# A two-layer attention stack on one NeuronCore: another table for the order, engines and buffers of the same operations

## The chip, the cores and the metric

The kernel runs on one core of a Trainium2 chip. A core has engines with instruction streams of their own: PE (TensorE, matrix products), ACT (ScalarE), DVE (VectorE), POOL (GpSimd) and SP (SyncE, which here only issues transfers). They meet at semaphores. The metric is the device time of one execution in microseconds. The kernel before took 455.38 us in the median of three runs (454.83 to 461.96).

## The reference

One sequence of 2048 rows of 512 elements in bf16 goes through four blocks A, B, A, B, each behind a layer norm and added to its input. Both have 32 heads of 16 columns.

```python
# A: attention in 4 segments of 512 rows, with a memory M, z carried from segment to segment
logits = einsum('bhqd,bhkd->bhqk', qs, ks) * scale + mask     # causal inside the segment
p = softmax(logits); a_dot = einsum('bhqk,bhkd->bhqd', p, vs)
num = einsum('bhld,bhde->bhle', phi(qs), M)                    # phi(t) = t+1 if t>0 else exp(t)
den = einsum('bhld,bhd->bhl', phi(qs), z)[..., None] + 1e-06
o = g * num / den + (1.0 - g) * a_dot                          # g = sigmoid(beta), per head
M = M + einsum('bhld,bhle->bhde', phi(ks), vs); z = z + sum_l phi(ks)
# B: linear attention over all 2048 rows
phi_q = concat(softmax(q @ w_phi), softmax(-q @ w_phi)); phi_k likewise
kv = einsum('bhsf,bhsd->bhfd', phi_k, v); z = sum_s phi_k
o = einsum('bhqf,bhfd->bhqd', phi_q, kv) / (einsum('bhqf,bhf->bhq', phi_q, z) + 1e-06)
# after either: x = x + o @ wo
```

## The kernel before

The program is written as a graph of 2904 operations. `Graph.op` records for each the engines that may run it, what it reads and writes, and the tiles it opens; nothing is sent to an engine then. Helpers do the recording, so most instructions of the profile carry a helper's line:

- `mm` (L326) records a group of matrix products: scores S and Sd (pK, pQ), probabilities times values PV (pW, and p or pP), the normaliser Zq (Rz) and numerator N (Rkv) of block B's queries.
- `pair` (L341) records a projection in two operations, one for each half of the contraction; between them PE may run other products. The second half carries a wait on the first (`hard=o1`).
- `act` (L351) is an ACT function, nearly always an exponential out of PSUM. `evac` copies PSUM to SBUF on ACT (L359) or on DVE (L360): this is the main choice of engine that the table has. `kmask` (L686 DVE, L688 ACT) and the memsets at the start (POOL or DVE) have such a choice too.
- `tr` (L364) is a transposing transfer on SP; `tpe` (L380) a transposition by PE with an evacuation. `dma` (L368) writes the value rows to DRAM (v_rows) and brings them back spread over partitions (pW). `load` (L462) brings the inputs and weights in, WB_o, the last layer's output weight, in eight pieces.
- L795 adds a segment's memory (Macc), L961 is a residual sum, L1015 and L1012 sum the keys' weights, L929 is block B's transposition with its sum (otp), whose evacuation is called ote; otr is the transposition of an output, xnT that of a normed input (xnTe its evacuation), Km the key mask, Kev and Vev the evacuations of keys and values, BVe that of block B's values, BK, BV, BQ and Wo the projections.

Work is tiled in 128 rows by up to 1024 columns. PSUM is four tiles of 128 x 1024 f32 (D0 to D3); nearly every product goes through one of them, so a product can start only when the reader of that tile's last use is done. A of a segment, B's keys of the segment, then B's queries of all segments together with the next layer's first projections follow each other, and the table interleaves them.

`Graph.place` decodes the table: a global order of the operations, an engine for each, and a buffer for each tile. A tile that takes over a buffer must wait for the last users of the one before it (`t.base`). `Graph.emit` then cuts the global order into five streams, one for each engine, and gives each operation the waits that the orders so far don't already cover:

```python
order = [self.ops[i] for i in np.frombuffer(raw, "<u2", n)]
slots = dict(zip(tiles, raw[3 * n:]))
    o.seq, o.eng = k, ENGS[raw[2 * n + o.id]]
...
cand = [d for d in deps if (d is o.hard or not (d.kind == "c" and d.eng == "pe" and e == "pe")) and not covers(kn, d)]
```

Every engine, SP's transfers included, goes through its stream in order: an instruction that waits holds all that stand behind it.

Of the kernel before, what the change touches and what calls it, by code (L numbers as in the profile page):

```python
# [16 lines left out]
D = 512  # L17
H = 32
# [42 lines left out]
class Tile:  # L61
# [17 lines left out]
    @property  # L79
    def t(self):  # L80
        return self.pool.tensors[self.slot]
# [1125 lines left out]
c-q~01C%YvvUWtIvs$OSk8RtwZQHhO+qP}nwr$&fRlCpJnYnk?y!+O_-oMs;xqDYuRz^lfeDOu>tkrRVL1IV_0QI0g5Hx^>&<LVIV`u_Rp&2xXWDp(VLOiGjnV~wAhxkweBxHk<Py<Rq  # L1207
R%ih&p%o~o3AvyGRD^<12y#MeXal987PN&jPzl;W3@8f;pfD7H_Rs-pLs38|1~H*Bl!M~X5n@3d=mec1AtZwAkOQhfUFZ!dAr)BY0=Xdxe1{+K6RN^%2!uD_Krr-yx6l_1e1z067}CHX
0PG3_;3**Xhj-8qy1@__3Q6G^aOe&LAvfm1_wWfm!xtC@d9erdgo%(3d%-l!iNhcl22lp^1H$z%12@2Q3`c`dz)YMA&*23O#t9GvmOemn%m}&IJa`GOU?Y^kuP_|Oz$WO2{V|wAXex|`
qF4+^!Z%m~4n=}3Fb#&_e8|E!!*&<}L(z}6LP?wsJ760`qX9SvRzWHBCx**lCuD)yFbQYEK->iyRs+XbFc||eEzE!^7=%k9I*o<Xum;NGR1|1&5|qUPxEzXLK`e|FFdXK`wJ;3JVLm8>  # L1210
XQ4E%gF?6hD&k5Qj`MH?#-K_V4#vTJ91j675+}oc9EDThFzkl|cmy1bKnLI;B*f7eKt~}MBhnr?2{CCe&cWTV4`*Q_j75>i4`<^7*b9j<KkS1EI0iGpSk$O+F)YO;I2RjW6I_gouo^bR
g_sVSVpLd()$u$mz{6-TB}OKRXJ8fXqKP;T7r}Tez?R{1Jc3nlH>JWxSQ%?z3P_Dru`$NRwOA9Qz(qJf>o5vkfJ+buS5bXT$7*41tcwew9yZ5=6c^LOYKo76R0mt&IoOOXu^G0)E!Y}Q
;wjvSo6sMUV0es&$MFQV!M1n^{4oTh(sc->qZoh@@CNLm^SA@EvIH0rFW@oUircXr?xo|f4WnZkTtk=P3be<A7!5-)Hm#-b)B$(nYCMN~Fa{ojLwFX~;Ck$cJ@5>6!VTD(R$wGNjXg0L
uArTmo@HQdXcxxBmb8*mP-pCd4e26Y!pIm4yJCGxj@>XNMa5Rsi1twpN<}HK0bRzV7>D*#FYJwduqL&o+EkZnQ9FuDQLqjbWc6qX#iQJ;J6?q=cnvyJV!A;$X(@G~tGJ0aQv$k%*YPek
rzX^xhEgXQM$M=%wx=6-6K`P%+<|-8fjUwP8crjqDRrf5^cd4(H@c74X(Yv`6EKRN-~-HxPcb9Dz=!w@vtcGIK$-C+X2;&thk8;kDoCeb5GAB#G=Y{=dc2K~Fas8%@$?+W&^Q`MqbVJB
r~cHJ22ej*M`I}om7pWEo`%q1I!YVp4i=`8l!x7djg*Z|q)C*Wm7-&GoDNYA)`Jey7D`H~X&X(Zt@Ie4KoR<ciRc}D#*8d4drx0*I~8Kz@fGI4T=W+2P(GHM^3V@FOH=48zM<E+gU--h
+DRv<Fnde)=p@~z+famEp=30bp3!M4%F@s&x=P>h9G$02G>x9qbh=Ep=n%`qa<bc$kKW@0I?O&%F?vK<@Dlq>KauDuy}`@uF{Put^om~72TV^#*hf6d($YivK}G2+eW3jGg)&eFmYIE|
($tY9r@`zA{iGpmAmfyuU1NjT3lcPsGSWM|&fM}vFX;xGPYdWKW7L&(W8dfkNy-b~Nzp~hN(WeR%0$4BX<A6xs4O#dkPT%g*f3U(on&RHCmYE|u@P(r^<v#wZ$@l58^g-89;_l8&B{|5
%1*b~ZN}IDR)J2jiqwboW96tX%L6&75@n%dtUo)=j<cCGi)Pb4wx1PaIcO}q!ZK5FHjZ6ol6PWfSP7>1ImX#Nc8AR&!S1tCtTL5klD%R6>>+!=?y^Pnmd$04*hMyvy<&4IfZc>D^q9S7
# [80 lines left out]
```

## Time and profile before

| | before |
|---|---|
| runs, us | 454.83, 455.38, 461.96 |
| median, us | 455.38 |
| profiled execution: its span, us | 454.8 |
| instructions | 26184, of them 12085 products and 12085 weight loads on PE |
| busy: PE, ACT, DVE, POOL | 427.2, 420.9, 403.1, 58.4 us |

The span is that of the profiled execution, which has no time of its own beside it; it lies 0.6 us under the median. Times inside it count from its start. Busy times of one engine are the sum of its instructions, overlaps of pipelined products counted once. In rows of instructions, out<-in are tile names with the buffer's number left out; "[0.73 <-PE D L326]" says that the engine had been idle 0.73 us and what ended that: here a product of line 326 into a PSUM tile. "issue" stands where the profile shows nothing that was waited for. In rows of groups, the numbers behind the count are the busy time in us, the mean of one in ns, and the idle time just before them.

### The profile page before, as it was taken

To read this page: it belongs to the slowest core of one execution; us is meant where nothing else is said; L and a number is where in the kernel's file an instruction comes from. 1 tells how busy PE (TensorE), PEld (TensorE's weight loads), DVE (VectorE), ACT (ScalarE), POOL (GpSimd) and SP (SyncE) were. 2 spreads that over 40 slices of the span, in tenths; PEclk is the share of its full clock that TensorE was granted. 3 is DMA by queue.
4 is the path that set the end of the run, shared out by engine and by line. 5 is a ranking of instruction groups with operands and counts; after the bars stand their busy time and mean duration, and the time that the engine had idled before them with its cause. 6 is when DMAs were issued, how large, how long until landed. Compare 5 with 4: busy or idle time off the path is not lost.

```text
span 454.8 us, 26184 instructions
## 1 busy us (share of the span) xinstructions
PE 427.2 (94%) x12085; PEld 289.5 (64%) x12085; DVE 403.1 (89%) x766; ACT 420.9 (93%) x584; POOL 58.4 (13%) x146
## 2 busy tenths in 40 slices
PE   8999999999999989989999998999999988999787
PEld 4756667767766666655556666677677666765444
DVE  7999999998798978869999997999898896788897
ACT  5999999999999997899999999999899999699992
POOL 3411014010101101100330112020020020110000
PEclk9999999999999999999999999999999999999999
DMA  8976655564247212101255668436232414300355
GB/s 251 217 165 100 99 93 109 107 87 80 45 76 111 38 40 50 13 3 27 62 111 86 85 97 103 71 87 81 57 50 49 109 19 63 46 17 4 49 91 180
DMA packets 105167, 36.71 MB, mean 81 GB/s; under 512 B 91730, under 2 KB 105058, under 8 KB 105058
## 3 DMA queue, kind: packets, MB, share of 16 engines
q1 hardware_dynamic: 104226, 34.50, 42.9%
q8 instruction: 95, 1.56, 1.4%
q10 hardware_dynamic: 800, 0.52, 0.4%
q14 instruction: 14, 0.11, 0.1%
q0 software_dynamic: 32, 0.02, 0.0%
HBM read 10.76 MB, written 6.55 MB: 38 GB/s over the span
## 4 chain that ended last, share of the span: by engine, by line
PE 61%; ACT 20%; DVE 12%; issue 3%; DMA 3%; POOL 1%; DVEq 0%
PE D L341 38%; PE D L326 22%; ACT p L351 11%; ACT pP L351 7%; DVE X L961 2%; DVE pQ L686 1%; DVE p L1117 1%; DVE stats L599 1%; DMA pX<-p 1%; DMA p<-p 1%; ACT pS L351 1%; DVE p L620 1%; DMA X<-in_A_x_dram 1%; DVE pK L360 1%; DVE p L906 1%
## 5 line engine op out<-in xcount | busy, mean ns | idle before, releaser
L351 ACT ACTIVATE p<-D 128x1024 bf16<-128x1024 f32 (+1 forms) x256 | 225.6, 934 | 10.8 <-PE D L341 4.9
L351 ACT ACTIVATE pP<-D 128x640 bf16<-128x640 f32 (+2 forms) x192 | 149.5, 828 | 7.2 <-PE D L326 5.9
L326 PE MATMUL D<-pK,pQ 64*128 64x128 bf16 (+6 forms) x1792 | 112.0, 227 | 4.2 <-ACT p L351 1.0
L326 PEld LDWEIGHTS D<-pK,pQ 64*128 64x128 bf16 x1792 | 67.0, 93 | 40.2 <-ACT pP L351 8.5
L326 PE MATMUL D<-pW,pP 64*128 64x50 bf16 (+1 forms) x3072 | 84.0, 181 | 3.4 <-issue 2.7
L326 PEld LDWEIGHTS D<-pW,pP 64*128 64x128 bf16 x3072 | 68.6, 93 | 9.2 <-issue 3.8
L607 POOL TENSOR_SCALAR rstd<-mv 128x1 f32<-128x1 f32 x60 | 17.0, 288 | 340.8 <-DVE mv L600 340.4
L326 PE MATMUL D<-pW,p 64*128 64x50 bf16 (+1 forms) x2048 | 50.4, 181 | 0.4 <-DVE pQ L686 0.2
L326 PEld LDWEIGHTS D<-pW,p 64*128 64x128 bf16 x2048 | 44.3, 93 | 3.9 <-issue 1.1
L599 DVE BATCH_NORM_STATS2 stats<-X 128x6 f32<-128x512 bf16 x63 | 42.3, 679 | 1.9 <-DMA X<-in_A_x_dram 1.6
L961 DVE TENSOR_TENSOR X<-X,D 128x1024 bf16<-128x1024 bf16 (+1 forms) x36 | 39.2, 1096 | 5.1 <-PE D L341 4.6
L326 PE MATMUL D<-tri,rep 64*128 64x64 bf16 (+1 forms) x384 | 40.1, 197 | 0.0
L341 PE MATMUL D<-pX,WA_k 64*128 64x512 bf16 (+1 forms) x288 | 37.4, 353 | 1.0 <-issue 0.5
L341 PE MATMUL D<-pX,WA_q 64*128 64x512 bf16 (+1 forms) x288 | 37.7, 353 | 0.6 <-issue 0.6
L609 POOL TENSOR_TENSOR rstd<-rstd,mhalf 128x1 f32<-128x1 f32 x60 | 35.9, 604 | 3.4
L341 PE MATMUL D<-WB_k,pX 64*128 64x512 bf16 (+1 forms) x288 | 33.8, 352 | 1.1 <-DMA pX<-p 0.4
L341 PE MATMUL D<-WA_o,p 64*128 64x512 bf16 (+1 forms) x288 | 33.2, 352 | 1.6 <-issue 0.8
L1015 DVE TENSOR_REDUCE pS<-p 128x64 f32<-128x1024 bf16 x28 | 33.4, 1211 | 0.9 <-ACT p L351 0.9
L341 PE MATMUL D<-WB_v,pX 64*128 64x512 bf16 (+1 forms) x288 | 33.3, 352 | 0.0
L341 PE MATMUL D<-WA_v,pX 64*128 64x512 bf16 x256 | 33.2, 377 | 0.0
L341 PE MATMUL D<-WB_o,p 64*128 64x512 bf16 (+1 forms) x288 | 32.5, 353 | 0.4 <-ACT p L351 0.3
L341 PE MATMUL D<-pX,WB_q 64*128 64x512 bf16 x256 | 32.5, 376 | 0.3 <-ACT p L351 0.3
(123 smaller groups left out, 665.5 us busy)
## 6 DMA issues: line engine op xcount, KB each, us to landing
v_rows<-pV SPq DMA_DIRECT2D x16, 272.0 KB, 3.6
pW<-v_rows SPq DMA_DIRECT2D x64, 68.0 KB, 2.7
out_dram<-X SPq DMA_DIRECT2D x7, 256.0 KB, 2.6
X<-in_A_x_dram SPq DMA_DIRECT2D x3, 512.0 KB, 7.7
pX<-in_B_wqkv_dram SPq DMA_DIRECT2D x3, 512.0 KB, 4.5
p<-p SPq DMA_TRANSPOSE x73, 3.2
pX<-p SPq DMA_TRANSPOSE x54, 3.6
WA_k<-in_A_wk_dram SPq DMA_DIRECT2D x2, 256.0 KB, 7.2
```

The source lines that it names most:

```text
L326: ins = e.matmul(out_ap, lhsT, rhs, start=st, stop=sp, tile_position=(basep(lhsT), basep(out_ap)))
L341: ins = e.matmul(out_ap, lhsT[64 * hf:64 * hf + 64], rhs[64 * hf:64 * hf + 64], start=k == 0 and i == 0, stop=k == 1 and i == len(lists[hf ...
L351: return self.g.op({"act": (dur, lambda e: e.activation(out_ap(), in_ap(), func, scale=scale))}, reads, writes, opens, label=label)
L360: "dve": ((340 if fast else n / 0.96 + 65), lambda e: e.tensor_copy(out_ap(), in_ap()))}
L599: v(lambda e: e.bn_stats(self.stats[:, t, :], self.X[:, t, :]), 602, [R("X", t)], [R("st", t)], label="bn")
L607: v(lambda e: e.tensor_scalar(rs, self.mv[:, t, 1:2], LN_EPS, None, op0=ALU.add), 170, [R("mv", t)], [R("rstd", t)], eng="pool", label="rstd")
L609: v(lambda e: e.tensor_tensor(rs, rs, self.mhalf[:], ALU.pow), 540, [R("rstd", t), R("mhalf")], [R("rstd", t)], eng="pool", label="rstd")
L620: v(lambda e: e.tensor_scalar(xn.t[:], self.X[:, t, :], self.mv[:, t, 0:1], self.rstd[:, t:t + 1], op0=ALU.subtract, op1=ALU.mult), 300, [ ...
L686: ch = {"dve": (129 + n / 3.84, lambda e, sl=sl, out=out: e.tensor_scalar(out(), src(), self.m4[:, sl:sl + 1], None, op0=ALU.mult))}
L906: v(lambda e, pvv=pvv, rden=rden, part=part: e.tensor_tensor(part(o).rearrange("p (a h d) -> p a h d", a=2, h=16), pvv()[:, :, :, 0:16], r ...
L961: self.v(lambda e: e.tensor_tensor(X(), X(), src(), ALU.add), 65 + 512 * n / 0.96, pr + xr, xr, label="res")
L1015: v(lambda e, E=E, k=k, Z=Z: e.tensor_reduce(Z.t[:, 64 * k:64 * k + 64], E.t[:].rearrange("p (a f h) -> p a h f", a=16, h=4), AX.X, ALU.ad ...
```

## The change

Only the string `ORDER` differs: the compressed table of order, engines and buffers. Operations, their dependencies, shapes and all functions stay as they are. The new table gives DVE 771 operations against 766 and ACT 580 against 583, since 15 operations go to another engine: seven from ACT to DVE, four from DVE to ACT, and four memsets between POOL and DVE. All the rest is order: on PE an operation stands on average 2 places from where it stood, on ACT 1, on DVE 6, on SP 4. Operations between the two halves of a projection are about as many as before.

```diff
 ORDER = """
-c-q~01C%YvvUWtIvs$OSk8RtwZQHhO+qP}nwr$&fRlCpJnYnk?y!+O_-oMs;xqDYuRz^lfeDOu>tkrRVL1IV_0QI0g5Hx^>&<LVIV`u_Rp&2xXWDp(VLOiGjnV~wAhxkweBxHk<Py<Rq
...
+c-rk+W3(;Fl8(qo*YP>mwr$(CZQHhO+qP}nw$az_soLlEd)@E#^t@TK=Es{gx!11BN(8?6B6j6k8z2S5h1?*aKE!|mKoAocG=Nxu5DywcBFF<45<_-q1o0s&C`bT}At8i76UYorAp$gmk`M^ZAvz?1
...
```

Three places show what moves. The rows are the streams as the engine gets them, without waits; the last number is the count of equal rows in a run.

PE at the last layer's queries (block B, 422 to 428 us in the trace of before): `Rz` rows are the normaliser Zq, `Rkv` rows the numerators N, `WB_q` rows halves of the query projection. Before:

```order
L326 MATMUL D<-Rkv,p 128x64 x16
L326 MATMUL D<-Rz,p 128x48 x12
L326 MATMUL D<-Rz,p 128x32 x2
L326 MATMUL D<-Rz,p 128x16 x2
L341 MATMUL D<-pX,WB_q 128x512 x8
L326 MATMUL D<-Rkv,p 128x64 x32
L341 MATMUL D<-pX,WB_q 128x512 x8
```

and after:

```order
L326 MATMUL D<-Rz,p 128x48 x12
L326 MATMUL D<-Rz,p 128x32 x2
L326 MATMUL D<-Rz,p 128x16 x2
L326 MATMUL D<-Rkv,p 128x64 x80
L341 MATMUL D<-pX,WB_q 128x512 x16
L326 MATMUL D<-Rkv,p 128x64 x16
L341 MATMUL D<-pX,WB_q 128x512 x8
```

The numerators that stood between the normaliser's groups and between the projection's halves are gathered into one run of 80 products ahead of the projections.

ACT at the value tile that leaves it (second layer, 361 to 368 us): `pT` is the evacuation of block B's values (BVe), `p<-D 128x1024` and `pP` rows are exponentials of scores. Before:

```order
L351 ACTIVATE pP<-D 128x4x160
L351 ACTIVATE pP<-D 128x4x192
L359 ACTIVATE pT<-D 128x16x64
L351 ACTIVATE p<-D 128x1024 x3
L351 ACTIVATE pP<-D 128x4x192
L351 ACTIVATE pP<-D 128x4x224
```

and after:

```order
L351 ACTIVATE pP<-D 128x4x192
L351 ACTIVATE pP<-D 128x4x160
L351 ACTIVATE p<-D 128x1024 x3
L351 ACTIVATE pP<-D 128x4x192
L351 ACTIVATE pP<-D 128x4x224
```

The evacuation is gone from ACT's stream (it stands on DVE's, behind a layer norm's statistics), and two exponentials change places.

DVE at the end of the program (444 us to the end): `L1117` multiplies a numerator by its weights, `L961` rows are the residual sums, the cast is an evacuation of a transposed output (ote). Before:

```order
L1117 TENSOR_TENSOR p<-p,pS 128x1024
L961 TENSOR_TENSOR X<-X,D 128x1024
L1117 TENSOR_TENSOR p<-p,pS 128x1024 x2
L961 TENSOR_TENSOR X<-X,D 128x1024 x3
L961 TENSOR_TENSOR X<-X,D 128x512 x2
```

and after:

```order
L1117 TENSOR_TENSOR p<-p,pS 128x1024
L961 TENSOR_TENSOR X<-X,D 128x1024
L1117 TENSOR_TENSOR p<-p,pS 128x1024
L961 TENSOR_TENSOR X<-X,D 128x1024
L360 CAST p<-D 128x2x4x64
L961 TENSOR_TENSOR X<-X,D 128x1024
L961 TENSOR_TENSOR X<-X,D 128x512 x2
```

The last multiplication now stands between the first two residual sums, and ACT's last evacuation but one has come in between the second and the third.

More of the change, by code (lines that the diff above doesn't have):

```diff
@@ L1211 @@
[L1211 to L1218, printed above, removed]
```

98 lines of the change are left out of this document (52 added, 46 removed).

## The prediction

> **What bounds the kernel now.** I read the page first: the span, each engine's busy time, and the engines' shares of the chain that ended last.
>
> ```profile
> span 454.8 us, 26184 instructions
> ...
> PE 427.2 (94%) x12085; PEld 289.5 (64%) x12085; DVE 403.1 (89%) x766; ACT 420.9 (93%) x584; POOL 58.4 (13%) x146
> ...
> PE 61%; ACT 20%; DVE 12%; issue 3%; DMA 3%; POOL 1%; DVEq 0%
> ```
>
> The span is 0.6 us under the median of the three runs (455.38) and equal to the lowest (454.83), so the sum below is made against 454.8 and carried over as it is. Three engines are nearly full, so the shares say little about where a microsecond is to be had. I therefore cut the span by windows at the places where the work changes. Columns: stretch, length, busy us and instructions of PE, PEld, DVE, ACT and POOL, the granted clock, DMA share, GB/s.
>
> ```profile
> 0.00:13.00 13.00, 11.14 (x183) 6.58 (x185) 9.74 (x32) 8.18 (x22) 4.66 (x24) 1.00 0.88 262
> 13.00:179.00 166.00, 159.06 (x4880) 111.59 (x4876) 151.89 (x286) 161.15 (x216) 24.08 (x53) 1.00 0.53 92
> 179.00:201.00 22.00, 21.63 (x421) 13.41 (x418) 18.64 (x40) 18.35 (x25) 1.57 (x4) 1.00 0.15 20
> 201.00:386.00 185.00, 175.14 (x5196) 119.10 (x5186) 166.16 (x308) 178.87 (x241) 24.83 (x57) 1.00 0.43 71
> 386.00:421.00 35.00, 33.63 (x742) 23.47 (x744) 28.75 (x54) 29.59 (x45) 3.22 (x8) 1.00 0.15 22
> 421.00:444.00 23.00, 19.07 (x564) 11.14 (x566) 20.50 (x41) 22.07 (x35) 0.00 (x0) 1.00 0.44 72
> 444.00:454.80 10.80, 7.49 (x127) 4.16 (x122) 7.45 (x9) 2.68 (x5) 0.00 (x0) 0.99 0.59 184
> ```
>
> In 13 to 179, 201 to 386 and 421 to 444 us ACT (exponentials of attention and feature maps) is busy 97, 97 and 96% of the time. Its idle time there is 166.00 - 161.15 = 4.85, 185.00 - 178.87 = 6.13 and 23.00 - 22.07 = 0.93, together 11.9 us of 374. In 179 to 201 and 386 to 421 PE is the full one (98 and 96%), idle 0.37 + 1.37 = 1.7 us. The operations stay the same, so this is the room: 11.9 us plus whatever work leaves ACT. A reordering can't gain much more; what it may lose has no such bound.
>
> The waits view says what makes up the idle time (engine, tile and line, released by whom: us, times, longest).
>
> ```profile
> PEld D L326 <- issue: 8.8, 17, 1.7
> PEld D L341 <- issue: 8.8, 23, 1.0
> ...
> ACT pP L351 <- PE D L326: 5.9, 15, 0.9
> ...
> ACT p L351 <- PE D L341: 4.9, 8, 1.7
> ...
> ACT p L351 <- PE D L326: 4.4, 11, 0.8
> ...
> DVE stats L599 <- DMA X<-in_A_x_dram: 1.6, 1, 1.6
> ...
> ACT p L636 <- DMA X<-in_A_x_dram: 1.3, 1, 1.3
> ...
> PEld D L341 <- DMA pX<-p: 0.6, 2, 0.3
> ```
>
> ACT waits for scores and projections that PE has not finished. Transfers are hardly waited for: outside the two input waits of the first 13 us only tenths are left.
>
> **Engine moves.** By the two tables 15 operations change engine, four of them memsets at the start. Seven PSUM evacuations leave ACT: two of transposed inputs (xnTe, 512 wide, at 7.7 and 221.7 us), one V (24.6), one pT value tile (BVe, 363.6), and two transposed outputs (397.0, 447.0); the seventh is a key mask (13.0). Four come to it: another key mask (12.9), a key copy (20.7), a transposed feature tile (30.9) and one memory sum (Macc, 263.4). Prices on ACT (busy us, mean ns, idle before), then on DVE (shortest, median and longest ns, first and last start):
>
> ```profile
> L359 ACT ACTIVATE pT<-D 128x1024 bf16<-128x1024 f32 x7 | 7.2, 1022 | 0.0
> L359 ACT ACTIVATE pX<-D 128x512 bf16<-128x512 bf16 x10 | 5.7, 596 | 1.3 <-PE D L380 1.3
> L359 ACT ACTIVATE p<-D 128x512 bf16<-128x512 f32 x7 | 4.2, 600 | 3.3 <-PE D L929 2.7 <-PE D L341 0.4
> L359 ACT ACTIVATE pV<-D 128x1024 bf16<-128x1024 f32 x3 | 3.2, 1064 | 0.0
> L351 ACT ACTIVATE pS<-D 128x256 f32<-128x256 f32 x8 | 3.1, 389 | 0.9 <-PE D L326 0.9
> ...
> L360 DVE CAST p<-D x17: 659/1220/1226, 20.7 to 432.3; 128x1024 bf16<-128x1024 f32 x11, 128x512 bf16<-128x512 f32 x6
> L360 DVE CAST pK<-D x16: 670/1224/1230, 13.6 to 340.3; 128x1024 bf16<-128x1024 f32 x13, 128x512 bf16<-128x512 f32 x3
> L360 DVE CAST pV<-D x13: 1196/1227/1227, 17.6 to 358.2; 128x1024 bf16<-128x1024 f32 x13
> L360 DVE CAST pT<-D x7: 1216/1218/1226, 102.1 to 378.6; 128x1024 bf16<-128x1024 f32 x7
> L360 DVE COPY p<-D x5: 375/425/427, 30.3 to 180.8; 128x512 bf16<-128x512 bf16 x5
> L360 DVE COPY MS<-D x4: 406/433/441, 34.4 to 264.1; 128x272 f32<-128x272 f32 x4
> ```
>
> In 201 to 386 ACT loses 0.60 (xnTe) and 1.02 (BVe). It gains Macc, whose form ACT never runs before: by the nearest row (256 f32 out of PSUM) it takes 0.39, by the 512-wide copy 0.60 at most; I take 0.4. Net -1.2. In 13 to 179 it loses 1.06 (V) and gains 0.60 + 0.60, net +0.1; the key masks cancel. The move at 397.0 lies in a stage where PE is full, the one at 447.0 in the tail. **Sum -1.1 us where ACT is the bound.**
>
> What pays is DVE: in 201 to 386 +1.22 (BVe) + 0.43 (xnTe) - 0.43 (Macc) = +1.2, in 13 to 179 +0.1 (1.23 for V, less a 512-wide copy of 0.43 and a key cast of 0.67). It has 18.8 and 14.1 us idle there, so the work itself is hidden; being in order, it can still be late with the tile that PE or ACT needs next. That is the second rival.
>
> In the tail ACT sat idle before its last two evacuations (the 2.7 us behind PE L929 above), so dropping one frees nothing. On DVE it now stands between two residual sums:
>
> ```profile
> 446.50 2.54 DVE L961 TENSOR_TENSOR X<-X,D 128x1024 bf16<-128x1024 bf16 x2
> 449.79 2.59 DVE L961 TENSOR_TENSOR X<-X,D 128x1024 bf16<-128x1024 bf16 x3 [0.74 <-PE D L341]
> ```
>
> That idle 0.74 us takes the evacuation, which is no dearer than about 0.7 us, so I put it at 0; if DVE gets there late it costs up to 0.7. The head and its input waits stay: 0.
>
> **Order on PE.** This is the larger term. I looked up, for every ACT wait over 0.2 us in the three ACT-bound stages, whether the products that PE runs just before the awaited one are the same in the new table. At 15 waits they differ: the first and the last of these are the two rows below, and together they are 6.3 us. At 6 waits, 2.1 us together, they are the same (114.31 and 360.31 are the first and last), and those I expect to stay; the 3.4 us left are gaps under 0.2 us.
>
> ```profile
> 31.23 1.41 ACT L351 ACTIVATE pP<-D 128x640 bf16<-128x640 f32 x2 [0.33 <-PE D L326]
> ...
> 425.05 0.38 ACT L351 ACTIVATE pS<-D 128x256 f32<-128x256 f32 x1 [0.73 <-PE D L326]
> ...
> 114.31 1.41 ACT L351 ACTIVATE pP<-D 128x640 bf16<-128x640 f32 x2 [0.33 <-PE D L326]
> ...
> 360.31 1.02 ACT L351 ACTIVATE p<-D 128x1024 bf16<-128x1024 f32 x1 [0.35 <-PE D L326]
> ```
>
> Bounds: at best all 11.9 us of idle time go; at worst as much is added as is closed, 0, or below it what DVE adds. I choose half of the 6.3, **-3.2 us**: a wait whose product is put ahead is closed, but what is put behind it is then the next to be late, and in stages that are 97% full there is little else to run there. Where the new order leaves the neighbours alone, as in both PE-bound stages apart from 384 to 394 us, I put it at 0 (bound: 1.7 us of PE idle time).
>
> The largest single place shows the kind of wait. ACT's 0.73 us above comes from PE:
>
> ```profile
> 424.77 0.24 PE L326 MATMUL D<-Rz,p 64*128 64x48 bf16 x7 [1.55 <-issue]
> q8 instruction: 95, 1.56, 1.4%
> ```
>
> PE stops for 1.55 us in the middle of one run of small products, waiting for nothing but "issue". The instruction queue moved 95 packets for 2 x 12085 PE instructions, some 254 each; the stop falls where such a packet ends in a stretch of 48-wide products, which PE gets through faster than the next packet comes. The new table has the same 24170 instructions, hence as many packets; it only decides what stands across each seam. In the rows of the order at that place the 48-wide products are followed by 80 of 64 columns, which are short as well, so I expect a stop there again, with another wait behind it. The value of moving seams is inside the -3.2, between 0 and the 0.73 + some tenths that reach ACT.
> The Trainium skill ("Runtime: NRT & Kernel Launch", Instruction fetch mechanics) says that code comes in blocks of 256 instructions and that crossing into the next costs one DMA tail bump, mostly hidden. The block size agrees with the 254 of this trace; "mostly hidden" does not fit 1.55 us of one row, and by it moving seams would be worth nothing at all.
>
> **Order on SP.** The value-row loads are now issued in fours after the transposes that were between them, and five pieces of the last weight (WB_o) earlier. What any of this can free is in the waits: 0.6 us on the transposes; what it can cost is a transpose queued behind loads that wait for the value rows to land.
>
> ```profile
> v_rows<-pV SPq DMA_DIRECT2D x16, 272.0 KB, 3.6
> pW<-v_rows SPq DMA_DIRECT2D x64, 68.0 KB, 2.7
> p<-p SPq DMA_TRANSPOSE x73, 3.2
> ```
>
> A transpose that stands behind such a load is held up to 3.6 us, one behind a group of four no longer than that since all four wait for one store. The new table mostly puts the transposes ahead of the group, into the landing time. 0, bounds -1 to +3.6 (one transpose late once).
>
> **The sum:** 454.8 - 1.1 - 3.2 = 450.5 us, 1.1% under the median. A difference under 2% (9.1 us) is about what a measurement of this kernel can't tell from none, so this counts as no change.
>
> **Rivals.**
> *Most of the idle time closes* (chance 0.16). For it: the waits are on PE, whose own dense work leaves room (busy rows overlap), and 15 of 21 places change. Against: DVE at 90% and four double PSUM tiles bind PE to the evacuations, and 3.4 of the 11.9 us are gaps under 0.2 us, too small to be one product out of place. If two thirds of the 11.9 go with the work of 1.1: 454.8 - 1.1 - 7.9 = 445.8, faster by 2.1%. All of it would be 441.8.
> *The waits only move* (0.22). For each one closed another opens, and a seam of the instruction stream falls at a worse place: one stop of 1.55 us more, and DVE's 1.2 us. Then 454.8 - 1.1 + 1.5 = 455.2, between 453.5 and 458. It is the fate of an order that is nearly balanced; what speaks against is that work does leave ACT.
> *DVE's queue becomes the bound* (0.05), the side of slower. DVE evacuates in order; each 1024-wide one takes 1.22 us, and a PSUM tile that comes free one place late holds up a score product and then ACT. Of such casts the rows above hold 44 (11 + 13 + 13 + 7). Were one in five late by its neighbour's 1.22 us and ACT waiting each time, that is 9 x 1.22 = 11 us: 454.8 - 1.1 + 11 = 464.7, slower by 2.0%. It decides once DVE is busy over about 97% of a stage; it stands at 90 to 92% and the moves add 0.7% in 201 to 386, hence the small chance.
> *The forecast* has the rest, 0.57.
>
> That the table would not do what it says is out: the two kernels run the same functions, and the tables' order is what is issued.
>
> **How the numbers follow.** The forecast case covers about 447 to 453.5. Faster by over 2% (under 446.3) holds only the first rival, with one case at its edge: 0.16. Slower by over 2% (over 464.5) holds only DVE's: 0.05. The rest, 0.79, is within 2%. The range of 8 in 10 takes the forecast's case, the moved waits up to 457, and of the closed ones those above 445: 445 to 457. Left out are about 0.09 below and 0.1 above.
>
> **What would show it.** ACT's busy time in 13 to 386 should fall by about 1 us and DVE's rise by 1.5. The row ACT pP L351 <- PE D L326 (5.9 us) should fall by a third; the ones at 114 and 360 us should stand. The issue rows on PE (8.8 and 8.8) should stay within 2 us of what they are, and a stop of over 1 us should still stand near 425 us. The tail from 444 us should still be 10.8 us, with DVE's 0.74 us filled. I am wrong if ACT's idle time in its stages is under 6 us (the first rival), or if a wait of ACT or PE on DVE L360 is among the top ten (the last).

## The result: the changed kernel is 1.0% slower

Over 20 runs each, the changed kernel takes 462.34 us in the median (459.62 to 464.78) against 457.01 (454.83 to 461.96). The ratio is 1.0101, interval 1.0073 to 1.0128: 4.6 us slower, between 3.3 and 5.9. Ratios here leave out the few executions in a slower state of the chip and medians do not, so a ratio is not quite the quotient of the two medians beside it (these differ by 5.3 us). The forecast was 450.5 us, range 445 to 457. The time of the execution whose profile follows was 460.22 us, its span 458.5: a span is 1.7 us less than the time that it belongs to, here and in the other executions that list both. The times of before differ a little between the sessions in which the runs below were taken (medians of 455.3 to 457.0 us), so each run has its ratio to the before of its own session.

The page of the changed kernel: span, busy times, and the engines' shares of the chain that ended last.

```profile
span 458.5 us, 26132 instructions
...
PE 428.9 (94%) x12085; PEld 290.9 (63%) x12085; DVE 404.6 (88%) x771; ACT 419.6 (92%) x581; POOL 58.1 (13%) x144
...
PE 65%; ACT 17%; DVE 9%; DMA 4%; issue 3%; SPq 1%; POOL 0%; DVEq 0%
```

ACT's work fell by 420.9 - 419.6 = 1.3 us and DVE's rose by 1.5, as the moves say. But a part of the chain has gone from ACT (20% before) and DVE (12%) to PE (61%). The stages by windows, with their borders put where the same operations stand now:

```profile
13.00:182.60 169.60, 158.75 (x4876) 111.70 (x4873) 151.29 (x283) 160.79 (x215) 23.77 (x51) 1.00 0.58 89
...
204.50:389.40 184.90, 174.37 (x5210) 118.74 (x5204) 167.48 (x310) 177.46 (x237) 23.50 (x56) 1.00 0.43 71
...
424.50:448.00 23.50, 21.10 (x525) 11.36 (x527) 20.47 (x42) 22.52 (x36) 0.00 (x0) 0.93 0.37 81
```

In the stages that ACT fills, its idle time is 8.81 + 7.44 + 0.98 = 17.2 us, where it was 11.9. The first of them alone is 3.6 us longer (169.6 for 166.0). The waits view of the changed kernel says what ACT and PE wait for:

```profile
PEld D L326 <- issue: 14.0, 24, 1.9
PEld D L341 <- issue: 12.3, 27, 1.6
PE D L326 <- issue: 9.7, 18, 1.7
...
ACT pP L351 <- PE D L326: 7.9, 14, 1.1
ACT p L351 <- PE D L326: 6.4, 14, 1.3
...
ACT p L351 <- PE D L341: 4.0, 8, 1.1
```

The weight loads' waits for "issue" were 8.8 + 8.8 = 17.6 us and are 26.3. (PEld is the weight load of a product, PE the product. A stop can be counted in a row of either, so from here on I give the PEld rows alone, L326 and L341 together.) ACT's waits for scores went from 5.9 + 4.4 to 7.9 + 6.4 us. Matched operation by operation, ACT's operations end 0.5 us later than before between 20 and 30 us, 2.6 at 40 to 50, 3.4 at 60 to 70, 5.5 at 120 to 130, 3.6 at 170 to 180 and 3.9 near the end (medians). By these two executions the loss begins in the first 60 us.

One place, PE and then ACT of the changed kernel:

```profile
33.80 0.33 PE L326 MATMUL D<-pK,pQ 64*128 64x32 bf16 x8
33.97 0.22 PE L326 MATMUL D<-tri,rep 64*128 64x128 bf16 x2
34.02 0.27 PE L326 MATMUL D<-pK,pQ 64*128 64x256 bf16 x1
35.95 0.38 PE L326 MATMUL D<-pK,pQ 64*128 64x256 bf16 x3 [1.66 <-issue]
...
36.37 1.02 ACT L351 ACTIVATE p<-D 128x1024 bf16<-128x1024 f32 x1 [1.21 <-PE D L326]
```

and PE of the kernel before, where the same number of its instructions has gone by:

```profile
32.69 1.01 PE L341 MATMUL D<-pV,p 64*128 64x136 bf16 x25
33.89 0.43 PE L341 MATMUL D<-pV,p 64*128 64x136 bf16 x7 [0.19 <-issue]
34.10 1.09 PE L341 MATMUL D<-WA_v,pX 64*128 64x512 bf16 x8
```

PE stops inside one group of four products, and ACT waits for that group. Counting PE's stream as it is issued (a product with its weight load is two instructions, a wait one), every stop over 0.4 us inside a group stands at the same place modulo 256, in both kernels: at the 193rd or 194th instruction. These are the ends of the packets in which the stream arrives (95 packets of the instruction queue in either kernel). Of the issue rows 10.3 of 17.6 us stand within three instructions of such an end before, and 19.6 of 26.3 us now; the rest stands elsewhere and did not grow. For each of the 94 ends I took the longest pause between two products next to it, less 0.1 us: together 15.1 us before, 20.8 now, 4.5 us of the difference at the first eleven ends.

So I also estimated the work that every packet holds: its groups of products, each at the shortest tenth of the times that this form takes in the trace of before. The "lack" below is the sum, over the packets, of what is missing to 3.7 us. By this estimate it is 24.9 us before (33 packets are short) and 27.7 in the changed kernel (42 are short): 2.8 us more, where the pauses grew by 5.7.

### The profile page after: what moved, and what is told of

Its sections match the earlier page's. It is cut to its first block, busy times and chain, and to the rows that moved or that the text cites. A ratio compares the mean times of both kernels' runs of the same rounds, so it can differ in the third digit from the quotient of the medians.

```text
span 458.5 us, 26132 instructions
## 1 busy us (share of the span) xinstructions
PE 428.9 (94%) x12085; PEld 290.9 (63%) x12085; DVE 404.6 (88%) x771; ACT 419.6 (92%) x581; POOL 58.1 (13%) x144
## 4 chain that ended last, share of the span: by engine, by line
PE 65%; ACT 17%; DVE 9%; DMA 4%; issue 3%; SPq 1%; POOL 0%; DVEq 0%
PE D L341 38%; PE D L326 26%; ACT p L351 10%; ACT pP L351 5%; DVE stats L599 2%; DVE X L961 2%; DMA p<-p 2%; ACT pS L351 1%; DMA v_rows<-pV 1%; DVE p L1117 1%; DMA X<-in_A_x_dram 1%; DVE p L620 1%; DMA pW<-v_rows 1%; SPq L368 0%; DVE p L1123 0%
## 5 line engine op out<-in xcount | busy, mean ns | idle before, releaser
L351 ACT ACTIVATE pP<-D 128x768 bf16<-128x768 f32 (+2 forms) x192 | 149.4, 823 | 9.5 <-PE D L326 7.9
L326 PE MATMUL D<-pK,pQ 64*128 64x128 bf16 (+6 forms) x1792 | 110.7, 227 | 7.7 <-issue 4.9
L326 PEld LDWEIGHTS D<-pK,pQ 64*128 64x128 bf16 x1792 | 66.5, 93 | 38.6 <-issue 5.4
L326 PE MATMUL D<-pW,pP 64*128 64x50 bf16 (+1 forms) x3072 | 85.4, 181 | 2.7 <-issue 1.7
L326 PEld LDWEIGHTS D<-pW,pP 64*128 64x128 bf16 x3072 | 69.6, 93 | 9.4 <-issue 3.3
L607 POOL TENSOR_SCALAR rstd<-mv 128x1 f32<-128x1 f32 x60 | 15.4, 262 | 344.3 <-DVE mv L600 344.3
L326 PE MATMUL D<-pW,p 64*128 64x50 bf16 (+1 forms) x2048 | 51.3, 181 | 2.3 <-issue 1.8
L326 PEld LDWEIGHTS D<-pW,p 64*128 64x128 bf16 x2048 | 45.1, 93 | 6.5 <-issue 2.5
L961 DVE TENSOR_TENSOR X<-X,D 128x1024 bf16<-128x1024 bf16 (+1 forms) x36 | 39.4, 1096 | 5.9 <-PE D L341 5.5
L341 PE MATMUL D<-pX,WA_q 64*128 64x512 bf16 (+1 forms) x288 | 37.8, 353 | 3.1 <-issue 1.4
L326 PE MATMUL D<-tri,rep 64*128 64x64 bf16 (+1 forms) x384 | 40.1, 197 | 0.3 <-issue 0.3
L341 PE MATMUL D<-pX,WA_k 64*128 64x512 bf16 (+1 forms) x288 | 37.0, 353 | 0.3 <-issue 0.3
L341 PE MATMUL D<-pX,WB_q 64*128 64x512 bf16 x256 | 33.8, 389 | 0.6 <-ACT p L351 0.5
L341 PE MATMUL D<-WB_k,pX 64*128 64x512 bf16 (+1 forms) x288 | 34.1, 352 | 0.2
L341 PE MATMUL D<-WB_v,pX 64*128 64x512 bf16 (+1 forms) x288 | 33.7, 353 | 0.4 <-issue 0.4
L341 PE MATMUL D<-WA_v,pX 64*128 64x512 bf16 x256 | 33.4, 377 | 0.4 <-issue 0.4
L341 PE MATMUL D<-WB_o,p 64*128 64x512 bf16 (+1 forms) x288 | 32.8, 353 | 0.8 <-ACT p L351 0.4
L341 PE MATMUL D<-WA_o,p 64*128 64x512 bf16 (+1 forms) x288 | 33.1, 353 | 0.4 <-DMA p<-p 0.4
```

The lines of the kernel that those rows point to most:

```text
L326: ins = e.matmul(out_ap, lhsT, rhs, start=st, stop=sp, tile_position=(basep(lhsT), basep(out_ap)))
L341: ins = e.matmul(out_ap, lhsT[64 * hf:64 * hf + 64], rhs[64 * hf:64 * hf + 64], start=k == 0 and i == 0, stop=k == 1 and i == len(lists[hf ...
L351: return self.g.op({"act": (dur, lambda e: e.activation(out_ap(), in_ap(), func, scale=scale))}, reads, writes, opens, label=label)
L607: v(lambda e: e.tensor_scalar(rs, self.mv[:, t, 1:2], LN_EPS, None, op0=ALU.add), 170, [R("mv", t)], [R("rstd", t)], eng="pool", label="rstd")
L961: self.v(lambda e: e.tensor_tensor(X(), X(), src(), ALU.add), 65 + 512 * n / 0.96, pr + xr, xr, label="res")
```

## The experiments

Theories: the **seam theory** (packets that hold too little work cost time at their ends), the **DVE theory** (the moved evacuations make DVE late), the **transfer theory** (SP's new order brings something late), later the **order theory** (products stand where they wait or are waited for) and the **spread theory** (the loss is not made at the start but all over the program). In the diffs of tables, old and new stand for the decoded tables of the two kernels.

### Half a packet more, the same order (e1, e2)

```diff
-            unit(64, 512, 1)
+            unit(64, *((64, 9) if k < 4 else (512, 1)))
```

> The changed kernel with 64 tiny products (128 PE instructions) in place of part of the warm-up at the start, of the same length in time. Everything behind them stands 128 places later in PE's instruction stream; order, engines and transfers are the changed kernel's. Seam theory (PE stops where a 256-instruction packet of its stream ends and the packet held less than about 3.7 us of work): counted from the two streams, the sum of work that short packets lack at 3.7 us is 24.9 us before, 27.7 after and 41.6 here, so this kernel should be 8 to 14 us slower than the changed one, about 470 to 476 us, with the issue waits of PE (25 us before, 39 after in the trace) above 45 us. DVE theory (the moved evacuations make DVE late) and transfer theory (the reordered transfers are late): no change against the changed kernel, 461 to 464 us.

> The kernel before with the same 64 tiny products in its warm-up, nothing else. Seam theory: the lack of short packets goes from 24.9 to 40.6 us, so 8 to 15 us slower than before, 465 to 472 us, though not one operation has moved; the old order loses its lead of 5 us on the new one shifted alike. DVE and transfer theory: as before, 456 to 459 us.

Measured: 473.8 us, ratio to before 1.0353 (1.0287 to 1.0419), and 473.04, 1.0362 (1.0314 to 1.0411). Behind the warm-up not one operation moved, and the kernel before lost 16 us, the changed one 11. The issue rows of the shifted kernel before:

```profile
PEld D L326 <- issue: 25.3, 35, 2.3
PE D L326 <- issue: 18.9, 21, 2.2
ACT pP L351 <- PE D L326: 17.6, 26, 2.5
...
PEld D L341 <- issue: 5.5, 19, 0.5
```

30.8 us where 17.6 stood; at packet ends 22.5 us for 10.3. The lead of the old order is gone once both are shifted alike. By the estimate of the lack, shifts of 32 to 224 instructions are worse than none for either table, and those of 8 no better: both tables fit their own packet ends.

### A whole packet more (e13, e14)

```diff
-            unit(64, 512, 1)
+            unit(64, *((64, 9) if k < 8 else (512, 1)))
```

> The kernel before with 128 tiny products (256 PE instructions, one whole packet) in place of part of the warm-up: twice the instructions that cost 16 us in the kernel before shifted by 128, but every packet end falls again on the products on which it fell before. Seam theory: 456 to 459 us, the 16 us are gone. If it was the added products themselves, or what the shorter warm-up does: 473 us or more.

> The changed kernel with the same whole packet. Seam theory: 461 to 464 us, as the changed kernel, against 473.8 with half a packet. Otherwise 474 us or more.

Measured: 458.05 us, ratio 1.0031 (0.9995 to 1.0067), and 460.39, 1.0076 (1.0036 to 1.0116). Twice the added products cost next to nothing when the ends fall on the old places. What cost 11 to 16 us in e1 and e2 is where the ends fall, not the products. The PEld rows agree: 14.4 and 25.9 us, near the 17.6 and 26.3 without the packet.

### What a packet costs by itself (e15)

```diff
-            unit(64, 512, 1)
+            unit(64, *((48, 1024) if k == 0 else (512, 1)))
```

> The kernel before with 2048 products of 48 columns (4094 instructions, 16 packets) put into its first warm-up step, so that PE does nothing but such products for the first 50 us and more; by their pace inside a run (26 ns) 128 of them take 3.3 us. Seam theory: PE stops at each packet end, every 128 products, and a packet takes its fetch time: about 3.5 to 4 us when no other transfer runs, more during the input loads of the first 12 us; 16 packets take 56 to 65 us, and the whole program 510 to 520 us. If packets cost nothing beside their products: no stops, 2048 x 26 ns = 53 us, 508 us.

Measured: 513.63 us in a single run, so it is the trace that counts here. PE's timeline, with nothing to do but such products:

```profile
8.54 2.05 PE L701 MATMUL D<-onesb 64*128 64x48 bf16 x128 [2.77 <-issue]
15.56 2.74 PE L701 MATMUL D<-onesb 64*128 64x48 bf16 x128 [4.97 <-issue]
19.29 2.75 PE L701 MATMUL D<-onesb 64*128 64x48 bf16 x128 [0.99 <-issue]
22.74 2.75 PE L701 MATMUL D<-onesb 64*128 64x48 bf16 x128 [0.71 <-issue]
...
55.20 1.78 PE L701 MATMUL D<-onesb 64*128 64x48 bf16 x128 [1.68 <-issue]
58.66 1.77 PE L701 MATMUL D<-onesb 64*128 64x48 bf16 x128 [1.68 <-issue]
```

PE stops after every 128 products, 256 instructions. From one start to the next it takes 3.45 or 3.73 us (19.29 to 22.74; 15.56 to 19.29), whether the products in it take 2.75 us or, later, 1.77: the time is the packet's, not the products'. While the input loads run (8.54 to 15.56) it is 7.0 us. The expectation's 26 ns a product is too long: 1.77 us for 128 at full clock is 13.8 ns, so without stops these products would have taken 28 us and not 53, and the two cases lie further apart than it said. The Trainium skill ("Runtime: NRT & Kernel Launch", Instruction fetch mechanics) says that the next 256 instructions are fetched while the present ones run, and that a crossing is mostly hidden. That the fetch goes on beside the work agrees with e15, where the step is the same for 2.75 and for 1.77 us of work. "Mostly hidden" holds for most of this kernel's packet ends, but at 12 of 94 before and at 18 in the changed kernel the pause counted above is over 0.4 us.

### The engines put back (e3)

```diff
-order, engines, buffers = new, new, new
+order, engines, buffers = new, old, new
```

> The changed kernel with the 15 operations back on the engines they had before; order and buffers are the new ones. DVE theory: the loss is won back, 456 to 459 us. Seam theory: PE's stream keeps its seams (lack 27.7 us as in the changed kernel), so 461 to 464 us, with ACT taking 1.1 us of work back. Transfer theory: 461 to 464 us.

Measured: 464.06 us, ratio 1.0149 (1.0066 to 1.0232). Nothing is won back, so the DVE theory falls. Its long stops stand at the changed kernel's packet ends again (1.60 us at the eighth, 1.12 at the twenty-first, against 0.22 and 0.21 before), so they belong to the order, not to one execution. The issue rows are 26.2 us, the changed kernel's.

### The transfers put back (e4, e12)

```diff
-order of SP's operations = new
+order of SP's operations = old (e4); old for the loads of inputs and weights only (e12)
```

> The changed kernel with the transfers of SP in the order they had before (all but 12 of 727 exchanged pairs are put back); the other engines as in the changed kernel. Transfer theory: most of the 5 us comes back, 456 to 459 us. Seam theory with fetches delayed only by the seams: unchanged, 461 to 464 us; if transfers that stand near a fetch slow it down, part of the stops before 60 us go, 1 to 3 us faster. DVE theory: unchanged.

> The changed kernel with its loads of inputs and weights on SP at the times they had before; transposes and value rows keep the new order among themselves, the other engines stay. If weights that arrive while packets of the instruction stream are fetched make the stops of the first 60 us longer: 1 to 3 us faster than the changed kernel, 459 to 461 us. If the stops come from what the packets hold alone: 461 to 464 us. Transfer theory after the failure of the old transfer order as a whole: a load that now comes late costs, 465 us and more.

Measured: 496.12 us, ratio 1.078 (1.0673 to 1.0888), and 462.75, 1.014 (1.0083 to 1.0197). The first is a miss the other way: the transfer order that served the old products starves the new ones. Two waits of PE in e4:

```profile
56.46 0.40 PE L326 MATMUL D<-p,pX 64*128 64x64 bf16 x8 [4.22 <-DMA pX<-pX]
65.46 1.09 PE L341 MATMUL D<-WA_o,p 64*128 64x512 bf16 x8 [3.79 <-DMA p<-p]
```

Transposes come late, as they do not with either own order: the new order of products needs the new order of transfers, so e4 can't say what that order costs by itself. Its issue rows are 43.4 us, but only 11.0 of them stand at packet ends.

The loads alone (e12) leave the time where it was, but not the trace. A stop of PE that is new in e12, and PE's rows at the place shown above, where the products stand in the same order:

```profile
20.62 0.27 PE L341 MATMUL D<-pX,WA_k 64*128 64x256 bf16 x1 [1.84 <-issue]
...
36.44 0.33 PE L326 MATMUL D<-pK,pQ 64*128 64x32 bf16 x8
36.61 0.22 PE L326 MATMUL D<-tri,rep 64*128 64x128 bf16 x2
36.66 0.45 PE L326 MATMUL D<-pK,pQ 64*128 64x256 bf16 x4
```

The stop of 1.66 us is gone, though the packet holds the same products; in the four other runs of the new order with the new loads there (e3, e11, e14, e16) 0.8 to 2.0 us pass between two products at this end, in e12 less than 0.1. Over the first eleven ends the pauses are 1.8 us in e12, 6.0 in the changed kernel and 1.5 before. From 13 to 30 us the DMA share is 0.69 in e12 and 1.08 in the changed kernel. So, by this one trace against five, loads that arrive beside the fetches are what makes the early stops longer: the work that a packet holds does not decide alone, how long the next one takes to arrive does too. The time did not follow, because the old loads are late for the new order: PE's weight loads stop 2.0 us near 20.6 us until the load of WA_q has landed, and 2.6 and 1.5 us near 64.7 and 250.6 us until transposes have. The profile calls these "issue" too: of e12's 25.9 us in the PEld rows 13.3 stand at packet ends.

### Products exchanged to fill the short packets (e5 to e8)

```diff
-order of PE's operations = new (e5, e6) or old (e7, e8)
+the same with 96 to 182 moves among neighbours that reduce the lack
```

> The changed kernel with 116 small moves in PE's order alone (products exchanged with neighbours, no product that ACT waits for more than 0.5 us of work later), chosen so that packets of 256 instructions hold more even work: what short packets lack at 3.7 us falls from 27.9 to 21.0 us. Nothing is added, and transfers and engines stay. Seam theory: 4 to 7 us faster than the changed kernel, 455 to 459 us. Order theory (the changed kernel is slow because products stand where ACT or DVE wait for them, and seams are only where this is seen): no gain, or a loss, 462 us or more.

> The same with freer moves (182, up to 1.0 us later for what ACT waits for, 3 us for the rest): the lack falls from 27.9 to 18.3 us. Seam theory: 5 to 10 us faster than the changed kernel, 452 to 458 us, if the later products cost ACT little. Order theory: slower than the first set of moves.

> The kernel before with 96 such small moves: lack from 25.0 to 21.1 us. Seam theory: 2 to 4 us faster than before, 453 to 455 us. Order theory: no gain.

> The kernel before with 161 freer moves: lack from 25.0 to 16.8 us. Seam theory: 4 to 8 us faster than before, 449 to 453 us. Order theory: slower than before, since products that ACT waits for stand up to 1 us later.

Measured: 495.67, 522.14, 477.24 and 510.92 us; ratios 1.0857, 1.1447, 1.0484 and 1.1219. All four missed by far, and by the count of moves rather than by the lack; all four came out as the order theory had said. The waits of e5:

```profile
ACT p L351 <- PE D L326: 22.9, 23, 4.3
PEld D L326 <- ACT p L351: 19.9, 30, 2.6
DVE X L961 <- PE D L341: 19.4, 15, 4.7
ACT pP L351 <- PE D L326: 18.8, 29, 2.3
PEld D L326 <- issue: 12.4, 21, 2.1
...
PEld D L341 <- issue: 11.6, 29, 1.2
```

The issue rows did shrink, 26.3 to 24.0 us, and those at packet ends from 19.6 to 9.7 (4.8 in e6; 5.6 and 2.8 in e7 and e8, for 10.3 before), but ACT's waits for scores rose from 14.3 to 41.7. I had limited how much later a product may stand and let it stand up to 3 us earlier: there it waits for ACT or DVE, and in PE's in-order stream all behind it wait too. No order was found in which the packets are filled without such waits, so these runs say nothing of what filled packets would gain.

### Old and new order joined (e9, e10, e11, e16, e17)

```diff
-order, engines, buffers = new
+order, engines, buffers = old up to 72 us (e9) or 123 us (e10) or 417 us (e17), new behind
+order, engines, buffers = new up to 128 us (e11) or 421 us (e16), old behind
```

> A table put together: what the kernel before does in its first 72 us in the old order, all the rest in the new order (the two orders have done the same products by then, so the packets behind stay within some instructions of the changed kernel's). By the two traces the changed kernel is 3.4 us behind at that point, and the stops at its first eleven packet ends are 4.5 us longer. Seam theory: the loss of the first 72 us goes, 457 to 460 us against 462.3 of the changed kernel. If the loss is not made there but spread over the program: 461 to 464 us. The joint can cost up to 2 us by other buffers.

> The same with the joint at 123 us, where the changed kernel is 5.4 us behind; from there to the end it wins 1.7 us back, since packet ends at 154 to 167 us stop PE for shorter. Seam theory: 462.3 - 5.4, about 457, at best 455 us, and faster than the table with the joint at 72 us. Spread theory: 461 us or more.

> The reverse: the new order until the same point, the old one behind it. Seam theory: 457 + 5.4, about 462 us, no better than the changed kernel, although nearly three quarters of the program are in the old order. Spread theory: 458 to 460 us.

> The new order until 421 us of the changed kernel, then the old order for the last 38 us: the numerators stand again between the normaliser's groups and the projection halves. In the changed kernel's trace the granted clock is 0.50 from 429 to 432 us, behind the gathered run of short products, and 16 projection products take 3.58 us there; in the trace of before it is 1.00. If the gathered run is what drops the clock: 1.00 here, and 1 to 2 us faster than the changed kernel less the longer stop near 428 us that comes back (1.55 against 0.52 us), so 461 to 462.5 us. If the drop comes by chance or from the seams: a drop here too.

> The reverse: the old order until 417 us, the new one for the last 38 us. If the gathered run drops the clock: about 0.5 for some 3 us near 428 us, and 0 to 1 us slower than before, 456.5 to 458 us, since the shorter stop gives back what the clock takes. If not: 1.00, and up to 1 us faster than before. If the loss that the second part of the program shows were all in this place: 2 us slower.

| | median, us | ratio to before | PEld issue rows, us |
|---|---|---|---|
| new throughout | 462.34 | 1.0101 (1.0073 to 1.0128) | 26.3 |
| e9, old to 72 | 464.17 | 1.0157 (1.0086 to 1.0227) | 19.4 |
| e10, old to 123 | 458.06 | 1.0047 (1.0015 to 1.0079) | 20.6 |
| e11, new to 128 | 459.28 | 1.0093 (1.0058 to 1.0129) | 20.7 |
| e16, new to 421 | 460.58 | 1.0119 (1.0063 to 1.0175) | 23.1 |
| e17, old to 417 | 457.61 | 1.0047 (1.0029 to 1.0064) | 13.7 |

The new first 128 us alone cost 0.9%, 4.2 us (2.6 to 5.9), nearly the whole loss, which is what the seam theory had said; by its time in us, 459.28, e11 would be the spread theory's, but the before of its session was faster too, 455.86. What stands behind 123 us costs 0.5%, 2.1 us (0.7 to 3.6), where the two traces had promised a gain of 1.7: one pair of executions is too little for that. That the two parts are together more than 4.6 us lies within their intervals. e9 is a miss, at about the time that the spread theory had for it (461 to 464 us): its stops are fewer, but the joint has a price of its own, among it a wait of 2.6 us of PE for a memory sum on DVE (L795), which is 0.2 us in the kernel before. None of the tables beats the kernel before.

e16 and e17 were meant for the clock. Windows of the changed kernel (the granted clock is the third number from the end):

```profile
424.50:428.50 4.00, 3.01 (x154) 2.40 (x156) 2.40 (x7) 4.00 (x10) 0.00 (x0) 1.00 0.03 8
428.50:432.50 4.00, 3.43 (x32) 1.04 (x28) 3.90 (x10) 3.85 (x6) 0.00 (x0) 0.57 0.30 59
432.50:436.50 4.00, 4.00 (x82) 2.21 (x80) 2.70 (x6) 3.30 (x5) 0.00 (x0) 1.00 0.50 100
```

and the products there, in the changed kernel and in e17, which has the same order at that place:

```profile
429.27 3.58 PE L341 MATMUL D<-pX,WB_q 64*128 64x512 bf16 x16 [0.51 <-ACT p L351]
```

```profile
424.04 2.14 PE L341 MATMUL D<-pX,WB_q 64*128 64x512 bf16 x16 [0.51 <-ACT p L351]
```

At half clock 16 products take 1.4 us more. With the old end (e16) the clock is 1.00 there, but also in e17, which has the gathered run. So the run of short products alone does not drop the clock. It fell there in all eight traces that have the new order at both ends (the changed kernel, e1, e3 to e6, e12, e14), and not in e9, e10 and e17, whose beginning is old. Other places have such stretches too, 3.4 us long or two or three times that, each behind 3.4 us in which PE was busy 71% or less (63% here; in e12 at 65.3 us, behind the wait for the transpose). That is not enough for a drop: from 421.4 to 424.8 us of the kernel before PE was busy 54%, and none followed. What sets it stays open. e17 is slower than before by as much as e10 is, which by its expectation would put the whole later loss into the last 38 us; but e16, without the new end, wins nothing, so this isn't settled either.

## Why the prediction was wrong, point by point

- **The base.** The sum started at 454.8 as if the span were a time. It is a span 1.7 us short of its time, and the median of 20 runs of before is 457.0 us. That is some 2 us of the error.
- **Engine moves, -1.1 us.** The work moved as reckoned: ACT -1.3 us, DVE +1.5. With the engines put back (e3) the time is neither better nor clearly worse: the freed microsecond did not reach the end.
- **DVE's tail and cover.** Held: the last evacuation is hidden, and DVE still waits 0.64 us for PE behind it (0.74 before); the stretch from the same operations on is 10.5 us for 10.8. The DVE rival is out by e3.
- **Order on PE, -3.2 us.** This is the step that failed. It took the waits of ACT for PE as the room, half to be closed. They grew: ACT's idle time in its stages rose from 11.9 to 17.2 us. The two waits expected to stay did: 0.33 us near 119 (114 before) and 0.31 near 364.
- **Inside that step, "the value of moving seams is inside the -3.2, between 0 and the 0.73 + some tenths".** The mechanism was seen, at the place near 425 us, and its size and sign were wrong. I looked at one long stop and at the ends that I knew, and set the rest at no change since the count of packets is the same. What counts is how much work each packet holds, and, in the first 60 us, which transfers run while the next one is fetched (e12): the stops at all packet ends grew by 5.7 us, the span by 3.7, and a shift of half a packet shows that this term can be 16 us. A warning was to be had before: by the estimate 33 packets with less than 3.7 us of work against 42.
- **The stop near 425 us.** Forecast over 1 us again; it is 0.52 us in the idle column near 427 us (1.55 before). The gathering helped there, and the half clock behind it took that back in this execution.
- **Order on SP, 0.** It asked only which transpose comes late, not what the loads do to the fetching of instructions. The new order of the loads lengthened the pauses at the first eleven ends from 1.8 us (e12) to 6.0; that e12 takes the same time all the same is two effects that cancel, not a term of nothing. And the bound of +3.6 us was far too small for a transfer order that doesn't fit: e4 is 7.8% slower than before, the changed kernel 1.0%, some 31 us between them.
- **The rival "the waits only move" (0.22).** Its mechanism, a packet end at a worse place, is the nearest to what the runs show. Its price, one stop of 1.55 us more, was not (its sum also leaves out the 1.2 us of DVE that it names): it is many small stops, and the case ended at 458 us where 462.3 was measured.
- **The signs.** Neither sign that was named for being wrong came: ACT's idle time rose, and no wait for DVE L360 is among the longest. What failed was a sign thought safe, the issue rows: they were to stay within 2 us and rose by 8.7.

What is shown is that the place of the packet ends decides over 11 to 16 us in either order (e1, e2, with e13 and e14 as the counter-test), that a packet takes 3.45 to 3.73 us whatever little it holds (e15), that transfers beside the fetch make the stops longer (e12), and that putting back engines or loads alone wins no time (e3, e12). That the loss of 4.6 us is made by these stops is argued, not shown. For it speak where they grew, their coming back in e3, and the rows (of one execution each, against medians): with 14 to 18 us in the PEld issue rows the time is 457 to 458 us (before, e13, e17), with 20.6 and 20.7 it is 458 and 459 (e10, e11), with 23 to 26 it is 460 to 464 (e16, e14, e3, the changed kernel), with 28.4 and 30.8 it is 474 and 473 (e1, e2); e9, e4, e12 and the exchanged products, which have waits of their own, stand apart. Against it speak e12, which takes the changed kernel's time with stops at its packet ends nearer to those of before, the lack, which differs by only 2.8 us, and e5 to e8, where the stops at the ends shrank and the order theory was right each time. How much of the 4.6 us is packet ends, and how much is products and loads that stand where they are waited for, stays open: no run fills just those packets and leaves the rest alone.

## What to carry to other kernels

When a kernel issues many short instructions on one engine, cut its stream into packets and compare the work in each with what a packet takes to arrive; count the short ones before and after a reordering, not only the longest stop, and look at which transfers run while a short one's successor is fetched. An order that fits its stream's packet ends fits them exactly: a changed count of instructions anywhere ahead moves every end behind it, so test a shift alone before blaming the new code. And the waits of an engine that is 97% busy need not be room: here they were to shrink by 3.2 us and grew by 5.3.

## What the runs showed that was not expected

A packet of 256 PE instructions takes 3.45 or 3.73 us with the transfers idle and 7.0 us beside the input loads, against a mean of 454.8 / 95 = 4.8 us that this kernel spends on one: the arrival of instructions is not far from a bound of its own. In e15 the granted clock fell to 0.50 while PE ran nothing but such products between stops:

```profile
12.00:24.00 12.00, 6.74 (x320) 6.49 (x321) 0.06 (x1) 0.00 (x0) 0.82 (x2) 0.50 0.21 56
24.00:36.00 12.00, 9.60 (x459) 9.21 (x452) 0.00 (x0) 0.00 (x0) 0.00 (x0) 0.50 0.02 4
36.00:48.00 12.00, 6.42 (x391) 5.95 (x384) 0.00 (x0) 0.00 (x0) 0.00 (x0) 0.81 0.02 4
```

It came back to 1.00 with no other work, at 40 us; the 48-wide products took 1.77 us for 128 then, for 2.75 at half clock. And exchanging PE's products by a few places, with everything else as it was, costs 20 to 60 us (e5 to e8), where all of ACT's idle time in its stages was 11.9 us before.
